# Inverse root mean squares of one batch by matmuls instead of spread by DMAs, in a kernel whose order of work is written out by hand

## The chip, the cores and the metric

The kernel runs on one NeuronCore of a Trainium2 chip. The metric is the device time of one execution in microseconds (us), as the median of several executions. An execution that the hardware profiler recorded is shown with it; its times are counted from the start of its span, which goes from the first to the last instruction.

## The reference

Two layers follow each other. The first is linear attention without a mask: for each of 8 batches and 8 heads, with 576 rows of 64 elements, `kv = kᵀv` and `out = q·kv`, and every row of `out` is divided by its root mean square and multiplied by a gain. The heads side by side give `x`, 576 rows of 512 elements in each batch. The second layer mixes each row with the row before it and runs a gated feed-forward:

```python
kv = np.einsum('bhsd,bhse->bhde', k, v)
out = np.einsum('bhsd,bhde->bhse', q, kv)
rms = np.sqrt(np.mean(out * out, axis=-1, keepdims=True) + 1e-06)
x = out / rms * g_norm            # then heads side by side: (8, 576, 512)
xk = mu_k * x + (1.0 - mu_k) * x_prev
xr = mu_r * x + (1.0 - mu_r) * x_prev
k = np.maximum(xk @ w_k, 0.0)     # 512 -> 1024
v = k * k @ w_v                   # 1024 -> 512
r = 1.0 / (1.0 + np.exp(-(xr @ w_r)))
return r * v
```

## The kernel before, in words

The first layer works by batches (0 to 7), the second by groups of 512 rows (0 to 8) that run across the batches: group g needs batch g and, for g from 1 to 7, also batch g-1. All matmul operands are bf16 and all accumulators are PSUM tiles called `ps`. There are four of these, of two banks each, for the whole kernel; a tile is handed out again once its last reader has been written down, and the new user then waits for that reader.

Nothing plans at run time. The kernel first collects *pieces* (`plan.add`), each with a name, an engine and the pieces it depends on. `plan.emit` then walks through the string ORDER and emits the pieces in exactly that sequence. So ORDER sets the queue of each engine: every engine takes its pieces in this sequence and waits at the head of its queue. A suffix @A or @D puts a copy or a scaling on ScalarE (ACT) or VectorE (DVE). The names, for a batch b, a half z of its head pairs (0 or 1; 01 is both), and a half i of its rows:

- `ld.kb`, `ld.vb`, `ld.qb` (L221, L226) load and cast to bf16. They are issued by GpSimd (POOL) and run one behind the other on its DMA queue; k, v and q have three tiles each, so a load also waits for the last reader of the tile it takes. `ld.wk`, `ld.wr`, `ld.wv` are the weights. `ldh.k`, `ldh.v` bring batch 0's first half in fp32 on SyncE's (SP's) queue, and `cst` casts it.
- `kv` (L274), `kc`, `ks` (L280), `kd`: `kᵀv` by TensorE (PE), copied, split, and copied again to the tile `kv`. `tq` (L367) transposes q on DVE. `u` (L291) is `q·kv`. `uc` scales it by the gain into the tile `uT`; `sq` (L389, ACT) squares it into the tile `sq`.
- The inverse root mean squares come in two ways, chosen by `CB`. For b < CB, `ssb.0` to `ssb.3` (L418) each multiply the tile `sq` with a 128x128 matrix of 1/64 in two matmuls of 288 columns, which leaves every row's mean of squares already on all the partitions that need it; a pass each on ACT, `rsb.0` to `rsb.3` (L297), writes 1/rms to the tile `rs`. For b >= CB, `ssb` (L398) makes eight matmuls with only 32 columns of weights, four of them side by side in the array; one pass `rsb` writes the tile `rsc`; and `spb.0`, `spb.1` (L440) are four DMAs each on SP's queue that repeat the rows of `rsc` over the partitions of `rs`. Batch 0 is done in quarters of its own (`ss0.zi`, `rs0.zi`, `mul0.zi`).
- `mul` (L411, L415), `d` (L309), `mk` and `mr`, `xk` and `xr` (L322, L329): x, its difference to the row before, the two blends. They run on DVE, `mk` and `mr` on DVE or ACT.
- In group g, `k` (L492, L517), `relu` (L475, ACT) and `ksq` (L532, DVE); `r` (L544) and `sig` (L554, ACT); `v` (L564), `out` (L577, DVE), and the stores `st` (L466, on SP's queue). `k2.6` is the seventh of eight column blocks of group 2, `v2.0.1` the second half of the sum for the first 128 of its rows.
- `z:512` and `zz` (L460) are matmuls with zeros that fill PE's queue at the start.

ACT works with two function tables: the inverse square root (`rs`) and the sigmoid (`sig`) are in different ones, and where the kind changes, a table load (L144) goes ahead. Batches 5 and 4 change places, so kv5 comes before kv4.

Of the kernel before, what the change touches and what calls it, by code (L numbers as in the profile page):

```python
# [8 lines left out]
BF16 = mybir.dt.bfloat16  # L9
# [22 lines left out]
class Plan:  # L32
# [3 lines left out]
    def add(self, name, on, fn, deps=(), bufs=(), also=None):  # L36
        assert name not in self.pieces, name
        p = self.pieces[name] = Piece(name, on, fn, deps, bufs, also)
        return p
# [17 lines left out]
def kernel(  # L57
# [15 lines left out]
    B, H, S, HD = q.shape  # L73
# [12 lines left out]
    RB = 4  # L86
    RING = RB * S
    NX = 4
    CB = 2
    X0 = 2  # L90

    const = ctx.enter_context(tc.tile_pool(name="const", bufs=1))
# [11 lines left out]
        "uT": (4, (128, 2, S), BF16),  # L104
        "sq": (3, (128, 2, S), BF16),
        "rs": (3, (128, 2, S), BF16),
        "rsc": (1, (128, S), BF16),
        "d": (2, (128, 2, S), BF16),
        "md": (4, (128, 2, S), BF16),
        "sqk": (2, (128, NFC, G), BF16),  # L110
# [38 lines left out]
    cols = const.tile([128, 9], FP32, name="cols")  # L149
    ones = const.tile([128, 128], BF16, name="ones")  # L150
    heads = const.tile([128, 32], BF16, name="heads")
    perm = const.tile([128, 2, 2, 128], BF16, name="perm")
# [188 lines left out]
    def attention(b):  # L341
# [41 lines left out]
        for z in range(NZ):  # L383
            for i, (c0, c1) in enumerate(PARTS):
# [6 lines left out]
                secs[(z, i)] = uc, sq_  # L391
        if b >= CB:
            psc, rsc = Buf("ps"), Buf("rsc")
# [12 lines left out]
        for z in range(NZ):  # L406
# [27 lines left out]
            ps_ = []  # L434
            if b >= CB:
                def spread(_, z=z, rs=rs):
                    for y in range(2):
                        for e in range(2):
                            r = 32 * (2 * z + y)
                            nc.sync.dma_start(out=get(rs)[64 * e:64 * e + 64, y, :],  # L440
                                              in_=rsc.t[r + e:r + 32:2, :].unsqueeze(1).to_broadcast([16, 4, S]))

                ps_.append(add(f"sp{b}.{z}", "S", spread, deps=[p_rsc], bufs=[rsc, rs]))
            for y in range(2 if b < CB else 0):
                ps = Buf("ps")
# [187 lines left out]
```

## Time and profile before

| what | value |
|---|---|
| median of 3 executions | 199.32 us (199.03 to 199.8) |
| the profiled execution | 199.39 us |
| its span, first to last instruction | 197.5 us |
| granted TensorE clock | 0.999 |
| PE busy | 188.0 us (95%), 1736 matmuls |
| DVE busy | 134.0 us (68%) |
| ACT busy | 127.0 us (64%) |
| function table loads on ACT | 12, 1.28 us each |
| `rs<-rsc` DMAs on SP's queue | 48, of 72 KB each |

The 1.89 us between the profiled execution and its span lie around the instructions. A busy PE is not an idle-free PE in this profile, because matmuls are pipelined and their ends are modelled; the times from one matmul's start to the next tell more. A matmul of 512 columns starts 0.216 us after the one before, so a piece `k`, `r` or `v` of four takes 0.863 us. The DMA share is over 1 where packets of several queues overlap on an engine.

### The profile page before, as it was taken

What the parts mean: (1) busy time and instruction counts of PE and PEld (TensorE: products, weight loads), DVE (VectorE), ACT (ScalarE), POOL (GpSimd) and SP (SyncE); (2) the same over time, 40 slices, a digit from 0 to 9 for tenths busy, and PEclk for the clock granted to TensorE, in tenths of its full rate; (3) what the DMA queues carried; (4) which work ended last, traced back from release to release, by engine and by line L of the source; (5) the groups of instructions that cost most, each with busy time, mean ns of one, the idle gap of its engine ahead of it and who ended that gap; (6) DMA issues with size and microseconds to landing.
All of it is one profiled execution on the core that took longest, in us unless ns stands there. A gap on an engine that the chain in (4) does not pass through costs nothing.

```text
span 197.5 us, 4233 instructions
## 1 busy us (share of the span) xinstructions
PE 188.0 (95%) x1736; PEld 93.2 (47%) x1760; DVE 134.0 (68%) x227; ACT 127.0 (64%) x166; POOL 24.6 (12%) x44
## 2 busy tenths in 40 slices
PE   7987999999998999999999999999999999999992
PEld 2445864443534544344556554444444444444451
DVE  3389979888749699964997949876398440431272
ACT  3365599569989579889895876795518463342300
POOL 7842433041303000000000000000000000000000
PEclk9999999999999999999999999999999999999999
DMA  6999999999999999999632404413506003002226
GB/s 219 214 206 216 198 198 208 212 204 214 212 238 263 225 233 280 229 214 262 251 110 60 113 5 113 131 37 81 150 0 240 25 0 110 0 0 106 94 90 244
DMA packets 21192, 30.63 MB, mean 155 GB/s; under 512 B 1964, under 2 KB 14516, under 8 KB 21172
## 3 DMA queue, kind: packets, MB, share of 16 engines
q0 software_dynamic: 11440, 16.19, 45.9%
q1 hardware_dynamic: 9588, 14.03, 22.0%
q8 instruction: 14, 0.23, 0.5%
q10 hardware_dynamic: 144, 0.13, 0.2%
q14 instruction: 6, 0.05, 0.1%
HBM read 33.56 MB, written 9.44 MB: 218 GB/s over the span
## 4 chain that ended last, share of the span: by engine, by line
PE 73%; DMA 14%; DVE 6%; ACT 2%; issue 2%; SPq 1%; POOL 0%; DVEq 0%; ACTq 0%
PE ps L517 25%; PE ps L564 25%; PE ps L544 12%; DMA q<-in_q_dram 11%; PE ps L460 4%; DMA rs<-rsc 3%; PE ps L492 2%; PE ps L291 2%; PE ps L274 2%; DVE xT L411 1%; DVE qT L367 1%; ACT relu L475 1%; DVE xk L329 1%; DVE d L309 1%; PE ps L398 1%
## 5 line engine op out<-in xcount | busy, mean ns | idle before, releaser
L564 PE MATMUL ps<-w_v,sqk 128*128 128x512 bf16 (+1 forms) x286 | 66.0, 373 | 1.0 <-issue 0.6
L517 PE MATMUL ps<-xk,w_k 128*128 128x512 bf16 (+1 forms) x280 | 59.1, 355 | 1.4 <-DVE xk L322 0.7
L475 ACT ACTIVATE relu<-ps 128x1024 bf16<-128x1024 f32 x36 | 36.7, 1025 | 24.4 <-PE ps L517 18.5
L564 PEld LDWEIGHTS <-sqk 128*128 128x128 bf16 x296 | 28.3, 98 | 32.6 <-issue 1.8
L532 DVE TENSOR_TENSOR sqk<-relu 128x1024 bf16<-128x1024 bf16 x32 | 21.6, 686 | 29.6 <-ACT relu L475 22.4
L517 PEld LDWEIGHTS <-w_k 128*128 128x128 bf16 x288 | 27.2, 98 | 27.9 <-issue 1.8
L544 PE MATMUL ps<-w_r,xr 128*128 128x512 bf16 x140 | 33.8, 379 | 0.2
L554 ACT ACTIVATE sig<-ps 128x1024 bf16<-128x1024 f32 x18 | 18.5, 1025 | 15.9 <-DVE out L577 7.8
L577 DVE TENSOR_TENSOR out<-ps,sig 128x1024 f32<-128x1024 f32 x16 | 19.5, 1219 | 11.2 <-issue 5.7
L389 ACT ACTIVATE sq<-ps 128x576 bf16<-128x576 f32 x32 | 20.2, 652 | 4.1 <-PE ps L291 2.2
L544 PEld LDWEIGHTS <-xr 128*128 128x128 bf16 x144 | 13.7, 98 | 16.0 <-issue 0.7
L367 DVE STREAM_TRANSPOSE qT<-q 128x576 f32<-128x576 f32 (+1 forms) x20 | 14.7, 761 | 3.7 <-DMA q<-in_q_dram 3.5
L144 ACT ACT_TABLE_LOAD x12 | 15.4, 1283 | 0.9 <-PEq L617 0.7
L134 ACT ACTIVATE md<-d,cols 128x576 bf16<-128x576 bf16 x20 | 14.2, 769 | 1.7 <-DVE d L309 1.5
L309 DVE TENSOR_TENSOR d<-xT 128x1152 bf16<-128x1152 bf16 (+1 forms) x18 | 12.4, 691 | 0.4
L134 ACT ACTIVATE uT<-ps,cols 128x576 bf16<-128x576 f32 x16 | 11.7, 744 | 1.2 <-PE ps L291 1.2
L415 DVE TENSOR_TENSOR xT<-uT,rs 128x1152 bf16<-128x1152 bf16 x14 | 10.4, 744 | 2.1 <-DMA rs<-rsc 1.1
L136 DVE TENSOR_SCALAR md<-d,cols 128x576 bf16<-128x576 bf16 x36 | 11.3, 363 | 0.2
L136 DVE TENSOR_SCALAR uT<-ps,cols 128x576 bf16<-128x576 f32 x12 | 9.6, 814 | 2.7 <-ACT sq L389 2.5
L322 DVE TENSOR_TENSOR xk<-md,xT 128x1152 bf16<-128x1152 bf16 x14 | 10.5, 756 | 1.2 <-ACT md L134 0.9
L322 DVE TENSOR_TENSOR xr<-md,xT 128x1152 bf16<-128x1152 bf16 x14 | 10.5, 748 | 0.5 <-ACT md L134 0.4
L460 PE MATMUL ps<-zero 128*128 128x512 bf16 x28 | 9.3, 477 | 1.5 <-DVE ident L167 1.2
(54 smaller groups left out, 121.4 us busy)
## 6 DMA issues: line engine op xcount, KB each, us to landing
out_dram<-out SPq DMA_DIRECT2D x35, 256.0 KB, 2.7
k<-in_k_dram POOLq DMA_DIRECT2D x6, 576.0 KB, 21.5
v<-in_v_dram POOLq DMA_DIRECT2D x6, 576.0 KB, 23.9
q<-in_q_dram POOLq DMA_DIRECT2D x6, 576.0 KB, 23.6
rs<-rsc SPq DMA_DIRECT2D x48, 72.0 KB, 4.2
w_k<-in_moe_w_k_dram POOLq DMA_DIRECT2D x2, 512.0 KB, 10.0
w_v<-in_moe_w_v_dram POOLq DMA_DIRECT2D x2, 512.0 KB, 15.0
k<-in_k_dram POOLq DMA_DIRECT2D x3, 288.0 KB, 12.9
```

The lines of the kernel that those rows point to most:

```text
L134: nc.scalar.mul(out=dst, in_=src, mul=col)
L136: nc.vector.tensor_scalar(out=dst, in0=src, scalar1=col, scalar2=None, op0=ALU.mult)
L322: nc.vector.tensor_tensor(out=dst[:, 2 * z:2 * z + 2, r0:r0 + w], in0=md.t[:, :, cs], in1=xT[:, :, cur], op=ALU.add)
L389: sq_ = add("sq" + name, "A", lambda _, ps=ps, sq=sq, cs=cs, w=w: nc.scalar.activation(out=get(sq)[:, :, cs], in_=ps.t[:, :, 0:w], func=AF ...
L460: nc.tensor.matmul(get(k_ps[(0, 0)])[:, 0, 0:n], zero[:, 0:128], zero[:, 0:n], start=not started, stop=not started)
L475: nc.scalar.activation(out=get(rt), in_=ps.t, func=AF.Relu)
L517: nc.tensor.matmul(get(ps)[:, fc % 2, a0:a1], w_k_sb[:, cc, 128 * fc:128 * fc + 128], xk[:, cc, x0:x0 + a1 - a0], start=(cc == 0), stop=(c ...
L532: nc.vector.tensor_mul(out=get(sqk)[:, 2 * f2:2 * f2 + 2, :], in0=rt.t, in1=rt.t)
L544: nc.tensor.matmul(get(ps)[:, ci % 2, :], xr[:, cc, n0:n0 + 128], w_r_sb[:, cc, :], start=(cc == 0), stop=(cc == NHP - 1))
L554: nc.scalar.activation(out=get(sg), in_=ps.t, func=AF.Sigmoid)
L564: nc.tensor.matmul(get(ps)[:, bank, cs], sqk.t[:, fc, 128 * ci:128 * ci + 128], w_v_sb[:, fc, cs], start=(fc == 0), stop=(fc == NFC - 1))
L577: dv = add(f"out{g}.{c2}", "D", lambda _, ps=ps, sg=sg, ot=ot: nc.vector.tensor_mul(out=get(ot), in0=ps.t, in1=sg.t), deps=ms + [sg_done], ...
```

## The change

`CB` becomes 3, so batch 2 now takes the first of the two ways: its `ss2`, `rs2`, `sp2.0` and `sp2.1` are replaced by `ss2.0` to `ss2.3` and `rs2.0` to `rs2.3`. The tile `rsc` gets two buffers. ORDER is replaced as a whole: the same pieces otherwise, four fillers fewer, 36 of the copies and scalings on the other one of ACT and DVE, and another sequence on every engine.

```diff
-    CB = 2
+    CB = 3
...
-        "rsc": (1, (128, S), BF16),
+        "rsc": (2, (128, S), BF16),
```

ORDER, cut to the stretches that matter here. The start:

```diff
-ldh.k ldh.v ld.q0.0 ld.q0.0b ld.q0.1b seta setp ident perm ld.k0.1 ld.q0.1 ld.v0.1 ld.wk0 ld.v1.1 ld.wk1 ld.k1.1 ld.q1.1 ld.k1.0 ld.v1.0 ld.wr
...
-cst.k0@D cst.v0@D cst.k1@A cst.v1@A [16 x z:512] kv0.0 kc0.0@A z:512 z:512 ks0.0 kd0.0@A tq0.0.0 tq0.0.1 z:512 z:512 u0.0.1 u0.0.0 tr9
...
+ldh.k ldh.v ld.q0.0 ld.q0.0b ld.q0.1b seta zz setp ident perm ld.k0.1 ld.q0.1 ld.v0.1 ld.wk0 ld.k1.1 ld.v1.1 ld.wk1 ld.q1.1 ld.v1.0 ld.k1.0 ld.wr
...
+cst.k1@A cst.k0@A cst.v1@D cst.v0@A [13 x z:512] kv0.0 kc0.0@A tq0.0.0 z:512 z:512 ks0.0 tq0.0.1 tr9 cols tq0.1.1 tq0.1.0 ld.q3.01 kd0.0@A u0.0.0
```

TensorE's queue (the words of ORDER that are PE's), from batch 0's second half on:

```diff
-u0.1.0 u0.1.1 k0.000 ss0.10 ss0.11 k0.010 k0.100 k0.001 k0.011 kv1.1 k0.101 ks1.1 k0.110 u1.1.0 u1.1.1 kv1.0 k0.111
...
-k1.4.1 ss2 k1.5.1 r1.2 kv3.01 r1.0 r1.3 ks3.01 r1.1 v1.1.0 u3.01.1 v1.0.0 v1.1.1 u3.01.0 v1.3.0 v1.0.1 v1.2.0 kv5.01 ss3 v1.3.1 v1.2.1 ks5.01 k2.4 k2.5 k2.2 k2.0 k2.1 kv4.01 k2.3 k2.6 ks4.01 k2.7
-r2.2 r2.0 r2.1 u4.01.0 r2.3 v2.2.0 v2.2.1 v2.1.0 v2.3.0 u4.01.1 v2.3.1 v2.0.0 v2.1.1 ss4 k3.2 k3.3 v2.0.1
+u0.1.0 u0.1.1 z:512 z:512 ss0.10 k0.000 ss0.11 k0.100 kv1.1 k0.010 ks1.1 k0.011 k0.101 k0.001 k0.110 u1.1.1 u1.1.0 k0.111 kv1.0
...
+k1.4.1 k1.5.1 r1.2 ss2.1 r1.3 ss2.2 r1.0 ss2.0 ss2.3 r1.1 kv3.01 v1.0.0 v1.0.1 ks3.01 v1.1.0 v1.1.1 u3.01.1 v1.2.0 v1.2.1 kv5.01 u3.01.0 v1.3.0 v1.3.1 ks5.01 k2.2 k2.3 k2.0 k2.1 kv4.01 ss3
+k2.4 k2.5 ks4.01 k2.6 u4.01.0 k2.7 v2.0.0 v2.1.0 u4.01.1 v2.2.0 v2.2.1 v2.0.1 ss4 v2.1.1 r2.2 r2.3 r2.0 v2.3.0 v2.3.1 r2.1 k3.2 k3.3 k3.4 k3.5
```

ACT's queue, then DVE's, then SP's, then POOL's, in the middle:

```diff
-relu1.1 rs2 uc2.10@A relu1.2 kc3.01@A sig1.1 sig1.0 sq3.11 sq3.01 uc3.01@A sq3.10 sq3.00 uc3.00@A uc3.10@A rs3 kc5.01@A mr2.0@A mr2.1@A relu2.2 relu2.0
+relu1.1 sq2.10 sq2.00 relu1.2 rs2.1 rs2.2 rs2.0 rs2.3 sig1.1 sig1.0 kd3.01@A mk2.1@A uc3.01@A sq3.01 sq3.11 sq3.10 uc3.00@A relu2.1 sq3.00 rs3 relu2.0
...
-mul2.1 d2.1 mk2.1@D xk2.1 mul2.0 d2.0 mk2.0@D xk2.0 kd5.01@D
+mul2.0 d2.0 mul2.1 kc3.01@D mk2.0@D d2.1 xk2.0 out1.0 uc3.11@D kc5.01@D xk2.1
...
-mul3.0 ksq2.3 d3.0 mr3.0@D mk3.0@D tq5.01.0 tq5.01.1 mul3.1 d3.1 xk3.0 mk3.1@D xk3.1 out2.1
+mul3.0 d3.0 mr3.0@D mk3.0@D xk3.0 mul3.1 d3.1 mk3.1@D xk3.1 xr3.0 out2.1 out2.0
...
-sp2.1 sp2.0 st0.3 st0.2 sp3.0 sp3.1 st1.2 st0.0 st1.3 st0.1 sp4.1 sp4.0
+st0.2 st0.3 sp3.0 st1.1 sp3.1 st1.0 st1.2 st1.3 sp4.1 sp4.0
...
-ld.k3.01 ld.v3.01 ld.q3.01 ld.k5.01 ld.v5.01 ld.k4.01 ld.v4.01 ld.q4.01 ld.q5.01 ld.v6.01 ld.k7.01 ld.q6.01 ld.k6.01 ld.v7.01 ld.q7.01
+ld.q3.01 ld.k3.01 ld.v3.01 ld.v5.01 ld.k5.01 ld.k4.01 ld.v4.01 ld.q4.01 ld.q5.01 ld.q6.01 ld.q7.01 ld.k6.01 ld.k7.01 ld.v7.01 ld.v6.01
```

## The prediction

> **What bounds the kernel now.** First the page's busy shares, then a table by stage (from PE's first steady matmul, to group 2, to the last matmul), then the longest PE wait and its chain.
>
> ```profile
> span 197.5 us, 4233 instructions
> PE 188.0 (95%) x1736; PEld 93.2 (47%) x1760; DVE 134.0 (68%) x227; ACT 127.0 (64%) x166; POOL 24.6 (12%) x44
> ...
> DMA  6999999999999999999632404413506003002226
> ```
> ```profile
> 0.00:18.25 18.25, 15.08 (x158) 7.38 (x161) 11.21 (x34) 9.13 (x15) 11.69 (x25) 1.00 1.01 213
> 18.25:63.96 45.71, 44.39 (x606) 23.89 (x612) 37.82 (x64) 36.90 (x53) 12.41 (x18) 1.00 1.18 216
> 63.96:193.60 129.64, 128.32 (x973) 61.97 (x988) 84.56 (x130) 80.97 (x100) 0.54 (x1) 1.00 0.47 124
> 193.60:197.50 3.90, 0.22 (x2) 0.00 (x0) 0.42 (x1) 0.00 (x0) 0.00 (x0) 0.93 0.59 208
> ```
> Columns: length, then busy time of PE, weight loads, DVE, ACT, POOL, granted clock, DMA share, GB/s. From 18.25 to 193.6 PE is full; no other engine is. So time is PE's work, what it waits, some 18 us of start and 3.9 us of end. DMAs are busy to 95 us but PE doesn't wait for them. The one long PE wait, from PE's timeline, and DVE's ahead of it:
>
> ```profile
> 63.96 0.82 PE L517 MATMUL ps<-xk,w_k 128*128 128x512 bf16 x3 [0.70 <-DVE xk L322]
> ```
> ```profile
> 57.92 0.76 DVE L415 TENSOR_TENSOR xT<-uT,rs 128x1152 bf16<-128x1152 bf16 x1 [1.12 <-DMA rs<-rsc]
> 58.72 0.76 DVE L309 TENSOR_TENSOR d<-xT 128x1152 bf16<-128x1152 bf16 x1
> 59.52 0.65 DVE L136 TENSOR_SCALAR md<-d,cols 128x576 bf16<-128x576 bf16 x2
> 60.20 0.76 DVE L322 TENSOR_TENSOR xk<-md,xT 128x1152 bf16<-128x1152 bf16 x1
> 60.87 0.75 DVE L415 TENSOR_TENSOR xT<-uT,rs 128x1152 bf16<-128x1152 bf16 x1
> ```
> ```profile
> 54.29 6.27 DMA rs<-rsc
> ```
> Group 2 waits for batch 2's chain, spread by DMA: rs2 ends at 49.70, the last of its eight spreads lands at 60.56 (the chain's 6.27 us). From a landing, mul, d, mk and xk take 0.75 + 0.76 + 0.65 + 0.76 plus gaps, 3.0 us. Batch 3's spreads, on SP's timeline, and the pass ahead of them:
>
> ```profile
> 49.73 5.97 SPq L440 DMA_DIRECT2D rs<-rsc  x8
> 55.80 1.41 SPq L466 DMA_DIRECT2D out_dram<-out  x2
> 62.07 5.81 SPq L440 DMA_DIRECT2D rs<-rsc  x8
> ```
> ```profile
> 60.01 1.28 ACT L144 ACT_TABLE_LOAD   x1
> 61.30 0.74 ACT L297 ACTIVATE rsc<-ps,eps 128x576 bf16<-128x576 f32 x1
> ```
> ```profile
> DMA to landing us min/median/max: 2.0/6.4/8.3
> ```
> rs3 ends at 62.05, 1.9 us *before* group 2 starts; sp3.1 lands at 75.62, 13.6 us after rs3; group 3 starts at 83.1. Nobody waits here. This spare time is what the change spends.
>
> **The change part by part**, as times in the new run. The sum is made against the profiled execution, 199.39 us, 0.07 above the median.
>
> *Start.* Before, 17 fillers (0.43 us apart until 5.85, then 0.22) hold PE until kv0.0 at 7.24, though the last cast ends at 6.67. 14 fillers end at 6.5, so kv0.0 starts at 6.75. Casts move between ACT and DVE, but the last still waits for `ldh.v` (landed 5.98). The chain kc, ks, kd, u, sq, ss, rs, mul, d, xk has the same rows in both and keeps 0.5 (xk0.00 done at 13.8 instead of 14.4). Two new waits eat later slack: k0.100 needs rs0.11's PSUM tile (ss0.11 after rs0.10 at 16.5, so 17.8; PE empty 1.0, against 0.99 + 0.64 lost near there before); and ld.wk1, moved behind ld.k1.1 on POOL's queue, lands at its 20.9, not 19.03, where xk0.10 is ready at 20.4. Summed so, g0's last `k` ends at 26.5 against 27.0, and group 1 starts at 39.5 against 40.0 (kv2.01, moved behind, taken out). I take -0.5; bounds -1.5 (k0.100's wait isn't there) and +0.5 (wk1's 1.9 us bites).
>
> *Batch 2.* ss2's eight matmuls take 0.36 us of PE (start to next start); two of L418's take 0.25, so four pairs take 1.0: +0.63, all on PE. ACT gets four passes of 0.74 for one, between relu1.2 and sig1.1. Queued behind them are sig1.1, sig1.0 and kd3.01; ss2.0 and ss2.3 wait for the PSUM of rs2.1 and rs2.2, kv3.01 and v1.0.0 for rs2.0 and rs2.3. r1.2, r1.3, r1.0 and r1.1 lie between and cover it: relu1.2 ends at 50.0, the passes at 50.7, 51.6, 52.7 and 53.3 (each starts 0.5 after its ss, or behind the last), and PE reaches v1.0.0 at 53.5 (thin; up to 0.7, one pass, if not). Eight DMAs leave SP's queue. mul2.0 starts at 52.8 instead of 60.87. On DVE out1.0 (after v1.1.1, 57.6) and kc5.01 (after kv5.01, 60.4) stand ahead of xk2.1, which ends at 61.6. From v1.0.0 PE has eight `v` (6.9), two `u` (0.76), kv5.01 (0.72) and two `ks` (0.78) to k2.2, 63.0 with the wait below: PE's wait of 0.86 (by starts) goes. New is ks3.01's wait for kc3.01, on DVE behind mul2.1: +0.2. ss3 (0.36) moves behind k2.1. So up to group 3: -0.5 + 0.63 - 0.86 + 0.2 = -0.5. Before, k3.2 starts at 83.1 with v2.0.1 (0.86) still to do, so 83.9 alike; the new PE can reach k3.2 at 83.4 (from 63.0: 20 pieces of 0.863, kv, ks, two ss and two u for 2.6, some 0.5 where small pieces change).
>
> *Batch 3, the step that decides.* On ACT, rs3 now stands behind relu2.1 and sq3.00, and relu2.1 needs k2.3. k2.3 ends at 64.7; relu2.1 (1.02) and sq3.00 (0.65) run to 66.5, the table load (1.28) to 67.8; PE's ss3 is done by 67.7. rs3: 67.85 to 68.6, which is 5.6 us *after* group 2's start. sp3.0 is issued from 68.6, a store of 256 KB (st1.1) next, then sp3.1. From rs to the last spread landed took 10.9 (batch 2), 13.6 (3) and 10.5 us (4), without a store between; st0.3 and st0.2 land 1.6 and 1.4 us apart. So sp3.1 lands between 68.6 + 10.5 = 79.1 and 68.6 + 13.6 + 1.5 = 83.7. Batch 3's own row is the nearest; its packets tell more. The first came 3.9 us after the issue, and under the loads one packet of a spread went out for each load packet: 40 per us beside q loads (4608 bytes), 88 beside k and v loads (1152 bytes). New: first packet at 72.5, 256 + 128 + 256 packets; ld.q7, now next to ld.q6, keeps the rate at 40 for 3 to 5.5 us, then 88; with 0.4 for completion that is 81.8 to 83.2. I take 82.3. xk3.1 is done 3.0 us later: k3.2 at 85.3, a wait of 1.9 (0 to 3.3 by the ends).
>
> By the Trainium skill, "DMA: Bandwidth & Descriptors", Specifications, a DMA from SP has a first byte after about 0.6 us. That would put the first packet at about 69.2 and the sum at 199.1, the second rival; the 3.9 us of this trace's row speak against it while loads run.
>
> *Behind it.* out2.1 is queued on DVE behind xk3.1 and xr3.0 and ends 2.0 us after k3.2's start; k3.4 needs its PSUM after 1.73: +0.25. v3.1.1 waits for ksq3.3: +0.2. Before, PE has no such wait after 64 us.
>
> *Covered moves.* st0.2 and st0.3 now run at 42 to 48 beside k3's and v3's loads (about 0.8 us each at the row's rate); v3 lands at 52.4 instead of 50.8, kv3.01 comes at 52.8: 0.4 covers it. POOL stops at ld.q7 until tq4.01.1 (about 69), with four k and v loads behind; ld.q6 keeps the queue full until 72, the last load lands by 94 as before, kv6.01 comes at 97: 3 us of cover, and what is late beyond it PE pays. sp4 stands behind three stores on SP's queue and lands by 93; k4.0 needs it at 101. Twelve table loads stay twelve. The end stays: the same last four pieces, stores as near.
>
> Sum: -0.5 + 1.9 + 0.45 = +1.85: 199.39 + 1.85 = 201.2.
>
> **The rivals.**
> - *Group 3's wait* (forecast), 201.2. For it: ACT's queue makes rs3 7.5 us later against group 2. Against: 4.3 us of spare time before (75.62 + 3.0 against 82.9) absorb most. Its own range is 199.9 to 203.0. Chance 0.62.
> - *The spreads stay hidden*: sp3.1 lands before 80.4, as batch 2's and 4's lag would allow. Then -0.5 + 0.2: 199.1. Against: both had no store between and fewer q packets beside them. Chance 0.22.
> - *Faster*: PSUM hands k0.100 another tile, or rs0.11 is early, and PE fills the start, gaining 1.5 rather than 0.5. It pulls rs3 along as PE gets ahead, so the wait stays the same size; with it 200.2, so it decides only from a gain of 3 us at k2.2 (60 instead of 63), or at 198.1 where the spreads also hide. For it: 3.4 us of PE gaps before 18.25. Chance 0.12.
> - *Loads late*: POOL's stop at ld.q7 empties the load queue for over 3 us and kv6.01 waits: 203.5 or more. Against: ld.q6 is in flight. Chance 0.04.
>
> **Numbers.** 0.5% (1.0 us) is about what a measurement of this kernel can tell from no change. Faster than 198.3 is the third rival and a little of the second: 0.13. Within, 198.3 to 200.3, is most of the second and the forecast's lower edge: 0.25. Slower is the rest: 0.62. The range reaches down to 198.6, under the hidden case, and up to 203.0 (the wait's upper end, 3.3 + 0.45 - 0.5 = +3.25, with 0.3 of the start's); 0.12 below, 0.06 above.
>
> **What would show it.** PE's first matmul of kv0.0 near 6.75. Four rows L297 into `rs` between 50 and 53.5 and 40 spreads in place of 48. Group 2's first matmul near 63 with no wait for `xk`. rs3 after a table load, ending about 5.5 us after it. mul3.1 with idle time before it ended by the DMA `rs<-rsc`, and k3.2 starting with a wait for DVE `xk` L322 of 1 to 3 us. Wrong if k3.2 starts without a wait, if PE waits elsewhere (for PSUM before 40 us, for `kv` loads near 95), or if rs2's passes stop PE at v1.0.0.

## The result

| | median | lowest to highest | executions |
|---|---|---|---|
| before | 199.44 us | 199.03 to 200.01 | 20 |
| after | 200.44 us | 199.50 to 203.59 | 20 |

The changed kernel takes 1.0054 of the time before, 95% interval 1.0034 to 1.0074: slower by half a per cent. Executions more than 1.5% above the fastest of their kernel are left out of all ratios, and of the medians of the experiments: 203.21 and 203.59 us here, two of six in e3. Without them the changed kernel still scatters more widely, over 2.7 us against 1.0. The profiled execution took 201.67 us, 1.2 above its kernel's median and 2.28 above the profiled execution of before. What the profile shows is therefore an execution that lost more than the median one.

The page of the changed kernel, its span, busy shares, and two groups:

```profile
span 199.9 us, 4227 instructions
PE 190.3 (95%) x1756; PEld 93.9 (47%) x1756; DVE 139.2 (70%) x243; ACT 119.9 (60%) x153; POOL 24.6 (12%) x44
...
L517 PE MATMUL ps<-xk,w_k 128*128 128x512 bf16 (+1 forms) x288 | 60.5, 356 | 2.2 <-DVE xk L322 1.9
...
L415 DVE TENSOR_TENSOR xT<-uT,rs 128x1152 bf16<-128x1152 bf16 x14 | 10.4, 748 | 4.3 <-DMA rs<-rsc 3.0
```

ACT has 7 us less to do and DVE 5 us more, PE's share is what it was. The line to look at is L517: its matmuls wait 1.9 us for `xk` at one place. The table by stage, cut at 62.90 us, half a microsecond ahead of group 2's first matmul (63.41), and at the end of PE's work, has the same columns as the one shown of before:

```profile
0.00:18.25 18.25, 15.28 (x158) 7.48 (x159) 11.05 (x33) 9.92 (x16) 11.71 (x25) 1.00 1.00 210
18.25:62.90 44.65, 44.06 (x599) 23.94 (x598) 39.15 (x65) 34.48 (x48) 9.41 (x14) 1.00 1.18 213
62.90:196.00 133.10, 130.86 (x1003) 62.47 (x1000) 88.58 (x146) 75.47 (x89) 3.51 (x5) 1.00 0.47 121
196.00:199.90 3.90, 0.07 (x1) 0.00 (x0) 0.42 (x1) 0.00 (x0) 0.00 (x0) 1.00 0.39 136
```

In the first two stages PE idles 3.6 us, where it idled 4.5 before. In the third it idles 2.24 us, where it idled 1.3. (The profile of before has no record of 24 of its 1760 matmuls, so its idle times are a little too large.) The last stage is 3.9 us in both. Group 2's first matmul comes at 63.41 us, where it came at 63.96 before. So the loss lies behind it. PE's timeline there, and DVE's ahead of it:

```profile
85.99 1.46 PE L517 MATMUL ps<-xk,w_k 128*128 128x512 bf16 x6 [1.88 <-DVE xk L322]
87.79 1.46 PE L517 MATMUL ps<-xk,w_k 128*128 128x512 bf16 x6 [0.35 <-DVE out L577]
```
```profile
78.83 0.76 DVE L415 TENSOR_TENSOR xT<-uT,rs 128x1152 bf16<-128x1152 bf16 x1 [2.53 <-DMA rs<-rsc]
79.62 0.76 DVE L309 TENSOR_TENSOR d<-xT 128x1152 bf16<-128x1152 bf16 x1
80.42 1.21 DVE L136 TENSOR_SCALAR md<-d,cols 128x576 bf16<-128x576 bf16 x4
81.67 0.76 DVE L322 TENSOR_TENSOR xk<-md,xT 128x1152 bf16<-128x1152 bf16 x1
82.90 0.76 DVE L415 TENSOR_TENSOR xT<-uT,rs 128x1152 bf16<-128x1152 bf16 x1 [0.48 <-DMA rs<-rsc]
```

Counted from the end of one matmul's slot to the next start, PE stands from 83.94 to 85.99 (2.05 us) inside k3.2, whose third matmul is the first that needs xk3.1, and for 0.51 us ahead of the first matmul of k3.4, whose PSUM tile out2.1 has still to read. DVE starts mul3.0 when sp3.0 has landed (after 2.53 us idle), and mul3.1 when sp3.1 has (after only 0.48). The chain of waits has that second landing as one step:

```profile
75.31 7.56 DMA rs<-rsc
```

And the way to it, on ACT and on SP's queue:

```profile
65.34 1.02 ACT L475 ACTIVATE relu<-ps 128x1024 bf16<-128x1024 f32 x1 [2.46 <-PE ps L517]
66.26 0.64 ACT L389 ACTIVATE sq<-ps 128x576 bf16<-128x576 f32 x1
66.92 1.28 ACT L144 ACT_TABLE_LOAD   x1
68.22 0.74 ACT L297 ACTIVATE rsc<-ps,eps 128x576 bf16<-128x576 f32 x1
```
```profile
68.98 3.73 SPq L440 DMA_DIRECT2D rs<-rsc  x4
72.81 0.58 SPq L466 DMA_DIRECT2D out_dram<-out  x1
73.43 2.48 SPq L440 DMA_DIRECT2D rs<-rsc  x4
```

rs3 stands behind relu2.1, which idles ACT for 2.46 us until group 2's own matmuls are there. It ends at 68.96, 5.5 us after group 2 started (63.41); before, it ended 1.9 us ahead of it. The last spread lands at 82.88, 13.9 us after rs3.

### The profile page after: what moved, and what is told of

The parts are those of the page before. It is cut to its first block, busy times and chain, and to the rows that moved or that the text cites. A ratio compares the mean times of both kernels' runs of the same rounds, so it can differ in the third digit from the quotient of the medians.

```text
span 199.9 us, 4227 instructions
## 1 busy us (share of the span) xinstructions
PE 190.3 (95%) x1756; PEld 93.9 (47%) x1756; DVE 139.2 (70%) x243; ACT 119.9 (60%) x153; POOL 24.6 (12%) x44
## 4 chain that ended last, share of the span: by engine, by line
PE 76%; DMA 11%; SPq 3%; POOL 3%; DVE 2%; ACT 2%; issue 1%; POOLq 0%; DVEq 0%
PE ps L564 28%; PE ps L517 25%; PE ps L544 14%; DMA w_k<-in_moe_w_k_dram 7%; DMA rs<-rsc 4%; SPq L440 3%; PE ps L291 3%; PE ps L492 2%; PE ps L274 2%; PE ps L418 1%; PE ps L280 1%; POOL q L232 1%; POOL k L226 1%; POOL v L226 1%; ACT L144 1%
## 5 line engine op out<-in xcount | busy, mean ns | idle before, releaser
L564 PE MATMUL ps<-w_v,sqk 128*128 128x512 bf16 (+1 forms) x296 | 67.5, 374 | 0.0
L517 PE MATMUL ps<-xk,w_k 128*128 128x512 bf16 (+1 forms) x288 | 60.5, 356 | 2.2 <-DVE xk L322 1.9
L517 PEld LDWEIGHTS <-w_k 128*128 128x128 bf16 x288 | 27.1, 98 | 29.2 <-issue 4.8
L544 PE MATMUL ps<-w_r,xr 128*128 128x512 bf16 x144 | 34.7, 379 | 0.0
L136 DVE TENSOR_SCALAR md<-d,cols 128x576 bf16<-128x576 bf16 x48 | 15.4, 365 | 0.3
L136 DVE TENSOR_SCALAR uT<-ps,cols 128x576 bf16<-128x576 f32 x13 | 10.6, 815 | 3.7 <-PE ps L291 2.0
L134 ACT ACTIVATE uT<-ps,cols 128x576 bf16<-128x576 f32 x15 | 11.2, 748 | 0.0
L297 ACT ACTIVATE rs<-ps,eps 128x576 bf16<-128x576 f32 x12 | 8.7, 743 | 1.0 <-PE ps L418 0.9
```

The source lines that it names most:

```text
L136: nc.vector.tensor_scalar(out=dst, in0=src, scalar1=col, scalar2=None, op0=ALU.mult)
L517: nc.tensor.matmul(get(ps)[:, fc % 2, a0:a1], w_k_sb[:, cc, 128 * fc:128 * fc + 128], xk[:, cc, x0:x0 + a1 - a0], start=(cc == 0), stop=(c ...
L544: nc.tensor.matmul(get(ps)[:, ci % 2, :], xr[:, cc, n0:n0 + 128], w_r_sb[:, cc, :], start=(cc == 0), stop=(cc == NHP - 1))
L564: nc.tensor.matmul(get(ps)[:, bank, cs], sqk.t[:, fc, 128 * ci:128 * ci + 128], w_v_sb[:, fc, cs], start=(fc == 0), stop=(fc == NFC - 1))
```

## The experiments

Two theories stood at the start. *W*: the loss is group 3's wait for batch 3's spreads, and it comes from rs3's new place and the store between them. *M*: it is something else, batch 2's three more passes on ACT and the 0.63 us that its matmuls take more on PE (eight in both ways), or the start, and the wait at k3.2 is absorbed behind it. Ratios are to the kernel before, run on the same chip (medians 199.62, 199.71 and 199.57 us). Diffs are of ORDER, cut to the words that move.

**e1, the store behind the spreads.**

```diff
- sp3.0 st1.1 sp3.1 ks4.01
+ sp3.0 sp3.1 st1.1 ks4.01
```

> The changed kernel with one word of the order moved: the store st1.1 behind sp3.1, so that batch 3's eight spreads go out together. Theory W (the loss is group 3's wait for batch 3's spreads): the store's 128 packets no longer lie between, sp3.1 lands about 1.4 us earlier, the wait at k3.2 (2.05 us in the profile) shrinks to some 0.6, and the time falls from 200.4 to about 199.6. Rival M (the loss is the 0.63 us of added matmuls and small waits all over the new order): no change, 200.4. Rival L (the spreads land when the loads let them, whatever stands between): sp3.1 lands as before, no change.

Measured: 200.15 us, ratio 1.0028 (1.0011 to 1.0045), profiled at 200.59. The gain is smaller than expected, and the interval overlaps the changed kernel's (1.0034 to 1.0074). PE's wait at k3.2 is 0.78 us (83.83 to 84.61), not gone. DVE's and PE's timeline of e1:

```profile
78.02 0.76 DVE L415 TENSOR_TENSOR xT<-uT,rs 128x1152 bf16<-128x1152 bf16 x1 [1.83 <-DMA rs<-rsc]
...
80.85 0.76 DVE L322 TENSOR_TENSOR xk<-md,xT 128x1152 bf16<-128x1152 bf16 x1
81.53 0.75 DVE L415 TENSOR_TENSOR xT<-uT,rs 128x1152 bf16<-128x1152 bf16 x1
...
84.61 1.46 PE L517 MATMUL ps<-xk,w_k 128*128 128x512 bf16 x6 [0.62 <-DVE xk L322]
```

mul3.1 has no bracket here: it waits for no DMA, but follows xk3.0 on DVE. What is left of the wait is set by the *first* spread: mul3.0 starts 78.02, the five passes up to mul3.1 take 3.51 us, from mul3.1 to xk3.1 done it is another 3.0. Taking the store away helps as far as that second chain allows, and no further.

**e2, rs3 and its spreads ahead of group 2.**

```diff
- uc3.00@A v1.3.0 ... kd5.01@D k2.2 k2.3 relu2.1 ... sq3.00 ss3 tq4.01.0 k2.4 k2.5 rs3 relu2.0 sp3.0 st1.1 sp3.1
+ sq3.00 uc3.00@A v1.3.0 ... kd5.01@D ss3 rs3 sp3.0 sp3.1 k2.2 k2.3 relu2.1 ... tq4.01.0 k2.4 k2.5 relu2.0 st1.1
```

> The changed kernel with sq3.00 moved ahead of uc3.00, and ss3, rs3, sp3.0 and sp3.1 ahead of group 2's first matmul (k2.2) and so of relu2.1. Theory W: rs3 ends near 65.6 instead of 69.0 (a table load still goes ahead of it), the spreads have landed by about 79.5, k3.2 starts without a wait for xk, and k3.4's wait for out2.1's PSUM (0.5) goes too; the time falls to 199.0 to 199.4. PE may wait up to 0.3 for sq3.00 at ss3. Rival M: 200.4 as before, since PE's work is the same. Rival L: the spreads still land near 82, and the time stays near 200.4.

Measured: 199.15 us, ratio 0.998 (0.9966 to 0.9995), profiled at 198.99. ACT, SP's queue, DVE and PE of e2:

```profile
64.26 0.74 ACT L297 ACTIVATE rsc<-ps,eps 128x576 bf16<-128x576 f32 x1
```
```profile
65.03 5.14 SPq L440 DMA_DIRECT2D rs<-rsc  x8
```
```profile
75.87 0.72 DVE L415 TENSOR_TENSOR xT<-uT,rs 128x1152 bf16<-128x1152 bf16 x1
...
79.33 0.75 DVE L415 TENSOR_TENSOR xT<-uT,rs 128x1152 bf16<-128x1152 bf16 x1
```
```profile
83.16 3.62 PE L517 MATMUL ps<-xk,w_k 128*128 128x512 bf16 x16
```

Neither mul waits for a DMA, all eight spreads have landed by 74.4, and k3.2 to k3.5 run as sixteen matmuls in a row: both gaps, 2.05 and 0.51, are gone. out2.1 starts at 82.94, not 86.52, because it stood behind xk3.1 on DVE. Nothing of batch 2 or of the start was touched, and the loss is gone, so M falls. This kernel is also a little faster than the one before, by an interval that just excludes no change.

**e3, a second store between the spreads** (the opposite of e1).

```diff
- sp3.0 st1.1 sp3.1 ks4.01 st1.0
+ sp3.0 st1.1 st1.0 sp3.1 ks4.01
```

> The changed kernel with a second store (st1.0) between sp3.0 and sp3.1: the suspected cause doubled. Theory W: sp3.1 lands 1.3 to 1.5 us later, the wait at k3.2 grows to about 3.4 us, and the time rises to about 201.7. Rivals M and L: 200.4, no change.

Measured: 203.19 us (four executions), ratio 1.0176 (1.0144 to 1.0208), 2.7 us above the changed kernel. PE's timeline of e3, whose profiled execution took 205.62 us at a mean granted clock of 0.979:

```profile
87.93 4.43 PE L517 MATMUL ps<-xk,w_k 128*128 128x512 bf16 x10 [3.98 <-DVE xk L322]
```

In this execution the wait is 4.1 us (83.80 to 87.93), 2.1 us longer than in the changed kernel's. sp3.1 is issued 1.25 us later than there, its first packet comes at 80.95 instead of 78.96, behind the packets of both stores, and it lands at 84.77, 1.9 us later, where a store was expected to cost 1.3 to 1.5. The long wait has a second price: the ten matmuls of the line above take 4.43 us, 0.43 us from one start to the next, where six took 1.46 in the changed kernel. The profile's granted clock falls to 0.5 at 86.15, during the wait, and is back at 1.0 at 92.97; the matmuls between lose some 2.5 us by it. That belongs to this execution; the four behind the median ran at mean clocks of 0.992 to 1.0.

**e4, the method alone**: CB = 3 in the order of before, with the eight spreads' words left out.

```diff
- ss2 k1.5.1 ... r1.2 ... r1.0 ... r1.3
+ ss2.2 rs2.2 k1.5.1 ... r1.2 ss2.3 rs2.3 ... r1.0 ss2.0 rs2.0 ... r1.3 ss2.1 rs2.1
```

> The kernel before, its order kept, with only batch 2's way changed: four pairs of matmuls and four passes in the place of ss2, rs2, sp2.0 and sp2.1 (rs2.2 where rs2 was, the others behind r1.2, r1.0 and r1.3). PE gets 0.63 us more. Theory W: batch 2's factors are there by 54, group 2's wait of 0.86 goes, rs3 keeps its place ahead of group 2 and group 3 doesn't wait: 199.2 to 199.4, no worse than before. Rival M: the added matmuls cost what they are, 200.0 or more.

Measured: 201.02 us, ratio 1.0067 (1.0047 to 1.0087): a miss. PE no longer waits for batch 2 ahead of group 2, but PE's timeline shows two others in its place:

```profile
55.17 1.04 PE L564 MATMUL ps<-w_v,sqk 128*128 128x512 bf16 x4 [0.23 <-DVE sqk L532]
...
57.02 0.44 PE L291 MATMUL ps<-qT,kv 32*64 32x288 bf16 x12 [0.56 <-ACT sig L554]
```

By starts the two stand for 0.40 and 0.84 us. The second is ACT's doing: the four passes of 0.74 us hold it, sig1.1 comes at 55.94 instead of 52.93, and u3.01.1 waits for the PSUM that sig1.1 reads. The first is not. It waits for a square on DVE, behind a transpose of q3, which waited for its load. The longest wait of that kind (the last number), in the waits of before and then of e4:

```profile
DVE qT L367 <- DMA q<-in_q_dram: 3.5, 3, 1.9
```
```profile
DVE qT L367 <- DMA q<-in_q_dram: 4.8, 4, 3.4
```

`ld.v3` landed at 49.70 instead of 48.02 and `ld.q3` at 52.48 instead of 50.83. With batch 2's spreads gone from SP's queue, two stores were issued at 41.94 instead of 55.80, and their packets ran at 45 to 50, beside v3's load. So the method alone costs 1.4 us here. The time is what M allows (200.0 or more), but the 0.63 us of matmuls is less than half of it: the passes need the work that the new order puts around them, and even the freed queue had a price.

**e5, the order alone**: CB = 2 in the new order.

```diff
- ss2.1 ... ss2.2 rs2.1 rs2.2 ... ss2.0 ... rs2.0 ... ss2.3 ... rs2.3
+ ss2 rs2 sp2.0 sp2.1
```

> The changed kernel's order with batch 2 in the old way (ss2, rs2, sp2.0, sp2.1 at the places of ss2.1 and rs2.1): the new order without the new method. The new order has mul2.0 on DVE right behind ksq1.2, near 53, with kc3.01 behind it. If the order needs the method, DVE stands until the spreads have landed (8 to 11 us after rs2, so near 60), ks3.01 waits for kc3.01, and the time rises by 6 to 9 us to about 207. If the order is good in itself, 199 to 201.

Measured: 209.94 us (two executions, both at a mean granted clock of 0.975), ratio 1.0513 (1.0482 to 1.0544). DVE and PE of e5:

```profile
59.86 0.76 DVE L415 TENSOR_TENSOR xT<-uT,rs 128x1152 bf16<-128x1152 bf16 x1 [7.68 <-DMA rs<-rsc]
```
```profile
63.45 0.58 PE L280 MATMUL ps<-kvn,perm 128*128 128x128 bf16 x4 [7.77 <-DVE kvn L130]
```

mul2.0 is at the head of DVE's queue in the new order, and kc3.01 behind it; with spreads by DMA PE stands 7.9 us for kc3.01. As in e3, the clock falls during the wait, to 0.5 from 58.96 to 69.20 us, which the expected 207 did not have. Each alone is slower than the kernel before, so "what the method gained" has no number of its own here.

**e6, batch 3 by matmuls too**: CB = 4 in the new order, so no spreads are left ahead of group 3.

```diff
- ss3 tq4.01.0 k2.4 k2.5 rs3 relu2.0 sp3.0 st1.1 sp3.1 ks4.01
+ ss3.0 rs3.0 tq4.01.0 k2.4 k2.5 relu2.0 ss3.1 rs3.1 st1.1 ks4.01
...
- relu2.2 k2.6 ksq2.1 ksq2.0 u4.01.0 k2.7 sq4.10 sq4.00 v2.0.0
+ relu2.2 ss3.2 rs3.2 k2.6 ksq2.1 ksq2.0 u4.01.0 k2.7 sq4.10 sq4.00 ss3.3 rs3.3 v2.0.0
```

> The changed kernel with batch 3 also by matmuls (CB = 4): ss3.0 to ss3.3 and rs3.0 to rs3.3 between the pieces from ss3 to sq4.00, no sp3. PE gets 0.63 us more, ACT 2.2 us. Theory W: nothing is left to land, k3.2 starts without a wait, k3.4's wait goes; some 1.3 us of waits (in the median run) against 0.63 of matmuls, and perhaps 0.5 where ACT's passes hold up relu2.2: 199.6 to 200.2. Rival M (matmuls are what costs): 201.1 or more.

Measured: 201.44 us, ratio 1.0081 (1.0058 to 1.0104): a miss. k3.2 has no wait, but the passes stop PE earlier, as its timeline shows:

```profile
70.24 1.02 PE L517 MATMUL ps<-xk,w_k 128*128 128x512 bf16 x4 [0.36 <-ACT rs L297]
...
73.91 1.89 PE L564 MATMUL ps<-w_v,sqk 128*128 128x512 bf16 x8 [0.83 <-ACT rs L297]
```

Both users got a PSUM tile that an rs3 pass had still to read. By starts the two stand for 0.53 and 0.99 us, and the matmuls take 0.63 more: 2.15 us given for the 2.05 and 0.51 removed. The median, 1.0 us above the changed kernel's, is in the range that M named; what it lost is not shown, since the profiled execution (200.67 us) was the fastest of the six.

**e7, three more fillers** ahead of kv0.0, to see whether a late start reaches the end.

```diff
- [13 x z:512] kv0.0
+ [16 x z:512] kv0.0
```

> The changed kernel with the three fillers back that the change took out ahead of kv0.0. They end near 7.15 instead of 6.5, so kv0.0 starts near 7.2. If the start's gain is carried to the end (the prediction's term of 0.5), the time rises by 0.3 to 0.5 us to about 200.8. If it is lost where kv0.1 waits for its load (v0.1 lands near 12.0 in both), group 1's first matmul stays where it is, within 0.1 us, and the time at 200.4.

Measured: 201.25 us, ratio 1.0082 (1.0059 to 1.0106), above both expected numbers. Its interval overlaps the changed kernel's (1.0034 to 1.0074), and the profile says why it can't settle the point; PE's timeline of e7:

```profile
8.45 0.73 PE L274 MATMUL ps<-v,k 64*64 64x64 bf16 x35 [1.59 <-ACT v L128]
```

kv0.0 starts 1.4 us later than in the changed kernel, but the fillers had ended 1.6 us before: `ldh.v` landed at 7.71 us here and at 6.29 there. That is the load's scatter, not the fillers. Group 1 then starts at 40.66 instead of 40.20, and the wait at k3.2 is 2.02: of a start 1.4 us late 0.5 us reached group 1, and the wait kept its size.

**e8, q7 behind two smaller loads.** The prediction had sp3.1 late because a spread's packets take turns with q loads, whose packets are four times as large. Here `ld.q7` comes behind `ld.k6` and `ld.k7`.

```diff
- ld.q7.01 ld.k6.01 ld.k7.01 ld.v7.01 ld.v6.01
+ ld.k6.01 ld.k7.01 ld.q7.01 ld.v7.01 ld.v6.01
```

> The changed kernel with ld.q7 moved behind ld.k6 and ld.k7, so that batch 3's spreads run beside loads of k and not of q. If a spread's packets go out one for each load packet (40 per us beside q, 88 beside k), sp3.1 lands 1 to 2 us earlier, near 81.3, the wait at k3.2 shrinks to 0 to 1 us, and the time falls to 199.6 to 200.0. If the kind of load doesn't matter, 200.4. POOL also no longer stops for tq4.01.1 ahead of ld.k6 and ld.k7.

Measured: 201.93 us, ratio 1.0122 (1.0091 to 1.0153): a miss, slower still. PE's timeline of e8:

```profile
86.16 1.46 PE L517 MATMUL ps<-xk,w_k 128*128 128x512 bf16 x5 [2.22 <-DVE xk L322]
```

sp3.1 landed at 83.05, 0.2 later. Beside the k loads sp3.0 did go faster (74 to 91 packets per us, 36 to 38 beside q in the kernel before), but its first packet came only at 72.75, and at 78 to 82 q7 ran beside sp3.1. What was gained in rate was lost at the first packet and at the end. The edit changed more than the kind of load, too: `ld.k6` and `ld.k7` no longer stand behind q7, so four loads and not two were on their way when sp3.0 was issued. So the kind of load alone does not decide when sp3.1 lands.

**e9 and e10, the loads issued earlier and later.** In the changed kernel the packet records show one DMA of sp3.0 between 70.31 and 71.92, then no spread packet until 74.70. From 69.86 to 73.4 GpSimd issues `ld.q7` and four more loads. These two kernels move that issue, by moving the transpose of q4 that `ld.q7` waits for.

```diff
- kc4.01@D sq3.00 ss3 tq4.01.0 ... tq4.01.1 ld.q7.01
+ tq4.01.1 kc4.01@D sq3.00 ss3 tq4.01.0 ... ld.q7.01
```

> The changed kernel with tq4.01.1 ahead of kc4.01 on VectorE, so that ld.q7 and the four loads behind it are issued by GpSimd from about 68.1 instead of 69.86 us. In the changed kernel the second DMA of sp3.0 moves no packet until 74.3, about 1 us after GpSimd's last issue ends (73.4). If what SyncE issues is held while GpSimd issues, GpSimd ends 1.7 us earlier, the second DMA starts near 72.6, sp3.1 lands near 81.3, the wait at k3.2 shrinks from 2.05 to about 0.5, and the median comes to about 200.0 or below. If the packets only wait for their turn behind the loads' bytes (q6 until 72, then q7), the loads come in the same order at the same times, sp3.1 lands near 82.9 as now and the median is that of the changed kernel, 200.4 to 200.7.

```diff
- tq4.01.1 ld.q7.01 ld.k6.01 ld.k7.01 ld.v7.01 ld.v6.01 relu2.2 k2.6 ksq2.1 ksq2.0
+ relu2.2 k2.6 ksq2.1 ksq2.0 tq4.01.1 ld.q7.01 ld.k6.01 ld.k7.01 ld.v7.01 ld.v6.01
```

> The changed kernel with tq4.01.1 behind ksq2.0 on VectorE, so that ld.q7 and the four loads behind it are issued from about 71.1 to 74.6 us. If what SyncE issues is held while GpSimd issues, two or three DMAs of sp3.0 move their packets from 70 on without a pause, and those issued after 71.1 start near 75.6; sp3.1 lands at 82 to 84 and the wait at k3.2 is 1 to 3 us. If the packets wait for their turn behind the loads' bytes, the pause stays at 72 to 74.3, where q7 begins, and sp3.1 lands near 82.9. u4.01.0 needs tq4.01.1, which is done by 70.9, where the changed kernel starts it: nothing or 0.1 us by that. Median 200.3 to 201.2 by either, so the packets' times tell.

Measured: e9 200.7 us, ratio 1.005 (1.0038 to 1.0062); e10 201.18 us, ratio 1.0078 (1.0062 to 1.0095). The pause moves with the loads' issue, as the first theory said: in e9 the second DMA begins at 72.72 (expected 72.6), in e10 three DMAs go out from 69.98 to 72.26 without a pause, the new loads being issued from 70.91 on only. But e10's fourth DMA begins at 73.43, not near 75.6, and sp3.1 lands earlier than the 82 to 84 expected. sp3.1 lands at 81.26 in e9 and 81.18 in e10 instead of 82.88; but rs3 was also 0.8 and 0.7 us earlier there, so at most 0.8 to 1.0 us of it is the issue's place. e9's wait is not the 0.5 that was expected, and its median is the one that the second theory gave. DVE and PE of e9:

```profile
81.28 0.76 DVE L415 TENSOR_TENSOR xT<-uT,rs 128x1152 bf16<-128x1152 bf16 x1 [0.51 <-DMA rs<-rsc]
...
84.37 1.46 PE L517 MATMUL ps<-xk,w_k 128*128 128x512 bf16 x5 [1.07 <-DVE xk L322]
```

PE is there earlier as well (83.13), so 1.24 us remain, and the median is the changed kernel's. e10's wait at k3.2 is only 0.62, but PE pays at the loads:

```profile
84.29 1.46 PE L517 MATMUL ps<-xk,w_k 128*128 128x512 bf16 x5 [0.46 <-DVE xk L322]
...
96.53 1.42 PE L274 MATMUL ps<-v,k 64*64 64x64 bf16 x144 [0.67 <-DMA v<-in_v_dram]
```

The last load lands at 96.39 there, and kv6.01 waits 0.83 us for it: the loads could not be held back by another microsecond.

## Why the prediction was right, and where not

It said 201.2 us, slower; the median is 200.44, slower, and inside its range. By its own steps, against the profiled execution:

| step | predicted | profiled |
|---|---|---|
| start: group 1's first matmul (before 40.0) | 39.5 | 40.2 |
| batch 2's passes end; v1.0.0 | 53.3; 53.5 | 54.03; 54.36 |
| group 2's first matmul | 63.0 | 63.41 |
| rs3 ends | 68.6 | 68.96 |
| sp3.1 landed | 82.3 | 82.88 |
| k3.2's first matmul | 83.4 | 83.51 |
| xk3.1 there for PE | 85.3 | 85.99 |
| wait at k3.2 | 1.9 | 2.05 |
| waits behind it | 0.25 + 0.2 | 0.51 |
| loads: v3 landed; last load; kv6.01 | 52.4; 94; 97 | 52.47; 95.52; 97.49 |

*Group 3's wait*, the step that decides, held in place and cause. e2 and e3 show that it carries the loss: gone or longer, with the time following each way; e1, with a shorter wait, points the same way, but its time is not clear of the changed kernel's. Its size is in part luck: xk3.1 came 0.7 us later than worked out, and the first two matmuls of k3.2, which the prediction did not let run ahead, covered 0.4 of that.

*Start* is the step that failed: the term of -0.5 measured +0.2. xk0.00 came at 13.82, as worked out (13.8), but two waits stand behind it, on PE's timeline of the changed kernel:

```profile
18.08 1.03 PE L492 MATMUL ps<-xk,w_k 128*128 128x256 bf16 x8 [0.69 <-DVE xT L411]
...
21.60 0.61 PE L492 MATMUL ps<-xk,w_k 128*128 128x256 bf16 x4 [0.48 <-DMA w_k<-in_moe_w_k_dram]
```

The first is the new wait of k0.100 (0.85 by starts, predicted 1.0), but not for the reason given: it ends with mul0.10 on DVE (L411, done at 18.03), which reads a PSUM tile too, and rs0.11 ends only at 18.17. The second decides: `ld.wk1` landed at 21.56, not 20.9, and k0.011 waited 0.65 us for it. This wait was named, and sized at a landing that holds in some executions only. In the ten profiles with this start the load landed between 20.74 (e9) and 21.56, and in nine of them group 1 started 18.64 to 18.65 us behind it, at 39.39 to 40.20, whether kv0.0 came at 6.78 or at 7.67; only e7, with kv0.0 at 8.45, is later (19.1). So fillers taken out gain nothing there: the load sets group 1's start, and a landing at 20.9 would have given the predicted 39.5.

*Batch 2* came out as worked out or better: PE lost nothing at v1.0.0, no longer waits at group 2, and does not wait 0.2 us for kc3.01 either (ks3.01 follows v1.0.1 at once). From group 1's start to k3.2 it gained 0.4, where +0.63 - 0.86 + 0.2 makes a gain of 0.03. Part of the prediction's -0.5 up to group 3 is a reading: before, k3.2 starts at 82.83 and not at 83.1, so what compares with the new 83.51 is 83.69, v2.0.1's 0.86 added. PE was there 0.2 us earlier than before, not 0.5; the start's loss and batch 2's gain nearly cancel.

*Batch 3's landing* is right to 0.6 us, but not by the way it was derived. The first packet was put 3.9 us after the issue and came after 1.3; the 2.8 us pause behind the first DMA then took the gain back. The rate rule (40 per us beside q, 88 beside k) fits the kernel before (36 to 38 and 90 to 93), but not every run: in the changed kernel sp3.0's last three DMAs went at 51 to 65 beside k6's loads and the end of q7's, and in e2 six of the eight went at 145 to 221 beside q's. As the cause of the lateness it fell in e8. One chain was left out altogether: mul3.1 also stands behind mul3.0 to xk3.0 on DVE, 3.5 us, so a landing of sp3.0 at 78.8 alone puts xk3.1's end at 85.4, half a microsecond short of what happened. The store that the prediction blamed costs that half microsecond directly; what e1's profile gained beyond it came with sp3.0, which landed 0.8 us earlier. That is not shown to be the store's doing: sp3.0's pause was 1.3 us in e1 and 2.8 in the changed kernel, but 1.2 in e3, with two stores behind it.

By the Trainium skill, "DMA: Bandwidth & Descriptors", Specifications, a DMA from SP has its first byte after about 0.6 us. Counted from the start of SP's issuing record, which lasts 0.55 to 0.7 us itself, sp3.0's first packet took 1.3 to 4.0 us beside the loads, so no run here shows that figure there. The measurement decides, and the hidden case that followed from the figure did not occur.

*Behind it*, 0.51 against 0.45 is the right sum in another place: all of it stands at k3.4, where out2.1 starts 86.52 because mul3.1's wait pushed it back, and v3.1.1 shows no wait.

The terms measured make -0.2 (PE at k3.2) + 2.05 + 0.51 = +2.4, and the two spans differ by 2.4 (197.5 and 199.9), so nothing is left over. But that is an execution that lost more than most. The median loses 1.0, about half of the forecast 1.85. That the median execution waits less at k3.2 is argued, not seen, as only one was profiled. For it speaks e9's profile, which lies at its kernel's median and waits 1.24 us. The scatter says little: e2, where neither landing is on PE's path, scatters by 1.5 us, but so does e1, where they still are.

## What to carry to other kernels

When a chain of DMAs gets faster for one batch, look at what the freed order does with the next one: here batch 2's gain was paid out of batch 3's spare time of 4.3 us, because its small pass was queued on ACT behind work of the group that it had always run ahead of. Putting that pass, its square, its sums and its DMAs back ahead of that group turned 0.5% slower into 0.2% faster (e2). And where two landings feed one engine, count from both: the later one is bounded below by the first one plus the engine's own chain.

## What the runs showed of the hardware

How long sp3.0 waits for its first packet goes with how many loads stand on the other DMA queue. Times in us from SP's issue of sp3.0 to its first packet, and what followed, from the packet records; the last column counts the loads that GpSimd had issued by then and that had not landed:

| kernel | issue | first packet | lag | pause behind the first DMA | loads |
|---|---|---|---|---|---|
| before | 62.07 | 65.87 | 3.8 | none | 8 |
| e4 | 64.35 | 68.32 | 4.0 | none | 7 |
| e2 | 65.03 | 68.99 | 4.0 | none | 3 |
| e8 | 68.81 | 72.75 | 3.9 | none; 0.4 behind the third | 4 |
| after | 68.98 | 70.31 | 1.3 | 2.8 | 2, five more from 69.86 |
| e1 | 68.86 | 70.20 | 1.3 | 1.3 | 2, five more from 69.75 |
| e3 | 68.83 | 70.26 | 1.4 | 1.2 | 2, five more from 69.71 |
| e7 | 69.44 | 70.77 | 1.3 | 2.9 | 2, five more from 70.32 |
| e9 | 68.17 | 70.26 | 2.1 | 0.4 | 2, five more from 68.65 |
| e10 | 68.31 | 69.98 | 1.7 | none; 1.2 behind the third | 2, five more from 70.91 |

With three loads or more the lag is 3.8 to 4.0 us and no pause follows behind the first DMA; with two it is 1.3 to 2.1, and a pause follows after the next loads have been issued. That holds in all ten profiles of the table. Once no load is left, the first spread of batches 5, 6 and 7 has a lag of 1.2 us in every profile. The number of loads alone is not the rule, though: sp4.1 of e4 was issued beside two loads and had a lag of 3.0. What makes the lag and the pause (the new loads being issued, or queued loads being served first) was not told apart and stays open.

A long wait of PE costs more than itself. Where it stood for 4.1 us (e3) and 7.9 us (e5), the granted clock fell to 0.5 during the wait and stayed there for 5.0 and 5.8 us of the work behind it, with 512-column matmuls 0.43 us apart. Waits of up to 2.4 us at k3.2 (e8) left it at 1.0. Where between 2.4 and 4.1 us it begins was not measured.

The other surprise is the start's scatter. `ldh.v`, which nothing of the edits touched, landed between 5.93 (e6) and 7.71 us (e7) across the twelve profiles, and `ld.wk1` between 20.74 and 21.56 in the kernels with the new start, so a start tuned to a few tenths of a microsecond can have a gain in some executions and none in others.
